# Turning two more attention heads through memory, contracting 128 rows for the others, and storing three results from another queue

## The chip, the cores and the metric

The kernel runs on one core of a Trainium2 chip. Its engines are PE (matmuls; PEld is its weight load), DVE (vector), ACT (scalar), POOL, and SP, which here only issues DMAs. The metric is the device time of one execution in microseconds. Before the change the median of three runs is 1002.09 us (1002.01 to 1003.88).

## The reference

Three layers follow each other, all in float32:

```python
# q, k, v: (4, 8, 576, 64); f: (4, 8, 576)
scores = scale * q @ k.T + (cum[:, None] - cum[None, :])      # cum = cumsum(log f), causal
attn = softmax(scores); o = attn @ v                          # 32 heads
x = o as (2304 tokens, 512)
h = maximum(x @ w_in, 0);  x = (h * h) @ w_out                # 512 -> 2048 -> 512
h = x @ w2_in;  out = (h - tanh(h)) @ w2_out                  # 512 -> 2048 -> 512
```

## The kernel before

**Precision.** Each float32 operand of a matmul is split into a rounded high part and a low rest, and a product is made of three matmuls: high by high, low by high, high by low. So PE runs 7144 matmuls, most of them 128 rows by 128 columns with 288 or 256 columns moving.

**Blocks.** The first MLP works on 8 blocks `j` of 288 tokens, each in 16 steps `i` over the hidden units. A step has 12 matmuls `hp` (line 168), the square of the ReLU on ACT with its rest on POOL or DVE, and, two steps later, 12 matmuls `yp` (line 197). The second MLP (the last stage, lines 1194 to 1480) multiplies by Strassen's scheme: 7 products for 8, with sums before and after. Attention is woven into blocks 0 to 5 so that PE has other matmuls to run.

**Attention in four forms.** Batch 0 (heads 0 to 7) comes in two parts: `first_a` before block 0 and `first_b` inside it. Heads 8 to `UT`-1 = 15 run in `attention()`: a generator that gives *pieces*, nine a head, each a few instructions. A head's scores `s_ps` (lines 538, 539) go to DVE (row minimum), ACT (exponential), POOL (normalising). The tile `P` is then transposed on PE (`trans`, lines 549 to 552: thirteen full transposes and two small ones), split into `PTh` and `PTl` by ACT and DVE, and multiplied with V (lines 609 and 614). 576 keys are 4 chunks of 128 and one of 64; the matmuls of the last chunk and the corner of the first 64 queries contract 64 rows. `advance` hands out pieces by half-steps: `cuts` and `ENDS` say how many by when (58 of the 116 by half-step 28 of block 0, the rest by half-step 26 of block 1).

**Turned heads.** From head `UT` on, DVE transposes blocks of 32 by 32 (`turn`) into `T`, `put` writes `T` to `p_d` in DRAM with four DMAs, and `get` reads it back, rearranged, into `PTl` with four more. ACT then rounds `PTl` to `PTh` (`p_high`), DVE takes the rest in place (`p_low`), and the same products follow (`pv_begin`, `pv_end`); here the rows beyond 64 are zeros and all matmuls contract 128. `plan_head` puts each of these into a *slot*, two to a step. Slot 0 is step 0 of block 2. A head has 7.75 slots (`PERIOD`), the first turned head starts at `START` = -4. At its slot a function runs either before the step's matmuls or, with `behind=True`, after them. The tile `PTl` has one buffer: `get` waits until the head before has been multiplied. Every second head is followed by `store_x` (lines 497, 498), two DMAs of the pair's outputs to `x_d`, from which `load_x` later fetches the tokens of a block.

**Order.** All DMAs but four small ones are issued by SP, in its program order, so one that waits holds up those behind it. For instructions emitted before step `MARK` (step 0 of block 2) the order on each engine is that of a scheduler's first pass; later ones stand as written.

**Before block 0** weights `w1` are widened and split for the first four hidden tiles (`split_a`, `split_b`, at the heads that `SPLIT_A` and `SPLIT_B` name) between the heads of `first_a`. The last pair of heads ends with the rounding of `xhl` (ACT) and its rest (POOL, line 433), which block 0's first step needs.

**The last stage** makes `gq` (DVE, POOL) in two buffers and stores each with one DMA `g_d<-gq` (`h_store`, line 1215). Step n+2 can write only when the store of step n has landed.

Of the kernel before, what the change touches and what calls it, by code (L numbers as in the profile page):

```python
# [16 lines left out]
B, H, S, D = 4, 8, 576, 64  # L17
# [8 lines left out]
LAG = 2  # L26
RING = 3
XLOADS = (((8, 0, 4),), ((11, 0, 3), (13, 3, 4)), ((13, 0, 4),))
F0 = 18
SLK = (None, 8)  # L30
MARK = (2, 0)
BUSY = (34, 2, 4, 6, 4, 0, 0, 0)
UT = 16
ENDS = (28, 26)
PERIOD = 7.75
START = -4
ENG = {
# [7 lines left out]
}  # L45
FETCH = {6: 4, 7: 5, 8: 6}
SPLIT_A = {4: 0, 6: 1, 8: 2, 9: 3}
SPLIT_B = {5: 0, 7: 1, 9: 2, 10: 3}
EARLY_SPLIT = 4
AHEAD_W = 3  # L50
W2EARLY = 6
TB = 288
NG = NF // 2
N2 = 288
# [15 lines left out]
def kernel(  # L70
# [10 lines left out]
    nc = tc.nc  # L81
# [23 lines left out]
    def by(name):  # L105
        return {"A": nc.scalar, "V": nc.vector, "P": nc.gpsimd, "S": nc.sync}[ENG[name]]
# [15 lines left out]
    def rest(eng, out, in_, hi):  # L122
        eng.tensor_tensor(out, in_, hi.bitcast(F32), ALU.subtract)  # L123
# [85 lines left out]
    def latest(engine):  # L209
        return next(x for x in reversed(nc.cur_bb.bb.instructions) if x.engine == engine)  # L210
# [118 lines left out]
    def first(h, part):  # L329
# [76 lines left out]
        def o_step():  # L406
            ps = bank0(part, "o_ps")
            t0 = tiles[0]
            for c in ((0, 2, 3, 4, 1) if part else (0, 2, 1)):
                if c == 4:  # L410
                    nc.tensor.matmul(ps[0:64, 128:256], vr[0:64, 4], ptr[0][:, 0:128], start=False, stop=False)
                    continue
                t = max(t0, c)
                nc.tensor.matmul(ps[0:64, (t - t0) * 128:256], vr[:, c], pt[0][:, c, t - 1:t0 + 1].rearrange("p t j -> p (t j)"),  # L414
                                 start=(c == 0), stop=(c == 1))
            if not part:
                ps0 = bank0(part, "o0_ps")
                nc.tensor.matmul(ps0[0:64, 0:64], vr[0:64, 0], ptr[0][:, 0:64], start=True, stop=True)
            e = h % 2
            if e == 0:  # L420
                XS[0] = two.tile([128, S], F32, tag="xs", name="xs")
            xs = XS[0]
            rr = slice(64 * e, 64 * e + 64)
            c0 = 320 if part else 64
            rounded(by("b_xs" if part else "a_xs"), xs[rr, c0:c0 + 256], ps[0:64, 0:256])
            if not part:
                rounded(by("a_xs0"), xs[rr, 0:64], ps0[0:64, 0:64])
            if e == 1:
                if part:
                    store_x(0, h // 2, xs, 320, S)  # L430
                else:
                    rounded(nc.scalar, X[0][0][:, h // 2], xs[:, :TB])
                    rest(by("a_xl"), X[0][1][:, h // 2], xs[:, :TB], X[0][0][:, h // 2])
                    rounded(nc.scalar, XE[:, 0, h // 2].bitcast(F32R), xs[:, TB:320])
                    rest(nc.gpsimd, XE[:, 1, h // 2], xs[:, TB:320], XE[:, 0, h // 2])
                    if h == H - 1:
                        for a in range(2):
                            nc.sync.dma_start(x_d[0][:, :, a, TB:320].rearrange("k p n -> p k n"), XE[:, a])
# [143 lines left out]
    def pv_parts(u):  # L582
        vh = VH.pop(u)
        b, h = divmod(u, H)
        e = h % 2
        ps = bank(u, "o_ps")
        if u < UT:
            hi, lo = (PT[k].rearrange("p q a s j -> p (q a s j)").rearrange("p (c t j) -> p c t j", c=4, t=4) for k in "hl")
            po = ps.rearrange("p (s j) -> p s j", s=4)
            at = lambda p, c, t: p[0:64, 3, 0] if c == 4 else p[:, c, t:]  # L590
            po_at = lambda t: po[:, t:]
            p0 = lambda p: p[0:64, 3, 1, :64]
            rows = 64
            seq = [(hi, 0), (hi, 1), (lo, 1), (hi, 2), (lo, 2), (hi, 4), (hi, 3), (lo, 3), (lo, 4), (lo, 0)]
        else:
            hi, lo = PT["h"], PT["l"]
            po = ps.rearrange("p (q s j) -> p q s j", q=4, s=4)
            at = lambda p, c, t: p[:, :, 2, 0] if c == 4 else p[:, :, c, t:]
            po_at = lambda t: po[:, :, t:]
            p0 = lambda p: p[:, 0:2, 3, 1]  # L600
            rows = 128
            seq = [(hi, 0), (hi, 1), (hi, 2), (hi, 3), (hi, 4), (lo, 1), (lo, 2), (lo, 3), (lo, 4), (lo, 0)]
        po4 = po[:, 3] if u < UT else po[:, :, 3]

        def products(a, z):
            for n, (pt, c) in list(enumerate(seq))[a:z]:
                t = max(0, c - 1)
                w, o = (vh[0:rows, c], po4) if c == 4 else (vh[:, c], po_at(t))
                nc.tensor.matmul(o, w.rearrange("p a d -> p (a d)"), at(pt, c, t), start=(n == 0), stop=(n == len(seq) - 1))  # L609

        def corner():
            ps0 = PS0[u] = bank(u, "o0_ps")
            for n, (a, p) in enumerate(((0, hi), (1, hi), (0, lo))):
                nc.tensor.matmul(ps0[0:64, 0:64], vh[0:rows, 0, a], p0(p), start=(n == 0), stop=(n == 2))

        xt = one.tile([64, 512], F32, tag="xsh", name="xt")

        def upper():
            rounded(nc.scalar, xt, ps[64:128])

        def out():
            if e == 0:
                XS[0] = two.tile([128, S], F32, tag="xs", name="xs")
            xs = XS[0]
            r = slice(64 * e, 64 * e + 64)
            if u < UT:
                nc.vector.tensor_tensor(xs[r, 64:], ps[0:64], xt, ALU.add)
            else:
                nc.vector.tensor_tensor(
                    xs[r, 64:].rearrange("p (s q j) -> p q s j", s=4, q=4),  # L630
                    ps[0:64].rearrange("p (q s j) -> p q s j", q=4, s=4),
                    xt.rearrange("p (q s j) -> p q s j", q=4, s=4), ALU.add,
                )
            rounded(by(pre(u) + "xs0"), xs[r, 0:64], PS0[u][0:64, 0:64])
            if e == 1:
                store_x(b, h // 2, xs, 0, S)

        return products, corner, upper, out
# [10 lines left out]
    def steady_init():  # L649
        for t in range(5):  # L650
            P[t] = one.tile([128, PT_SZ[t]], F32, tag=f"P{t}", name=f"P{t}")
            if t % 4:
                nc.gpsimd.memset(P[t][:, NKEY[t]:], 0.0)
        PT["h"] = one.tile([128, 4, 4, 4, 32], F32R, tag="PTh", name="PTh")
        PT["l"] = one.tile([128, 4, 4, 4, 32], F32R, tag="PTl", name="PTl")
        PT["t"] = one.tile([128, 4, 4, 4, 32], F32, tag="T", name="T")
        nc.gpsimd.memset(PT["t"], 0.0)

    def attention(u0):
        for p in range(u0 - 2, UT):  # L660
# [94 lines left out]
    def plan(slot, f, *a, behind=False):  # L755
        PLAN.setdefault(slot, ([], []))[behind].append((f, a))

    def plan_head(k):
# [38 lines left out]
        if new:  # L797
            plan(o + 5, turn, 2)
            plan(o + 5, turn, 1)
            plan(o + 5, turn, 0)  # L800
            plan(o + 5, put, k)
            plan(o + 6, get, k, behind=True)
        if k == UT + 1:
            plan(o, prep_v, UT)
        if k + 1 < NU:
# [17 lines left out]
    def weights_early(h):  # L823
        if h in FETCH:
            fetch_w(w1, FETCH[h], FETCH[h])
        if h in SPLIT_B:
            for s in range(2):
                split_b(SPLIT_B[h], s)
        if h in SPLIT_A:
            for s in range(2):  # L830
                split_a(w1, SPLIT_A[h], s, two, "QA", 2)

    TA = one.tile([128, 2048], F32, tag="T", name="TA")
    XE = TA[:, 1024:1280].rearrange("p (a k n) -> p a k n", a=2, k=NK)
    first_a(weights_early)

    def w1_ahead(i):
        if EARLY_SPLIT <= i + AHEAD_W - 1 < NF:
# [258 lines left out]
    later = []  # L1097
    for k in range(UT + 1, NU + 1):
        plan_head(k)
    for g in range(NB * NF + LAG):  # L1100
        j, i = divmod(g, NF)
        if (j, i) == MARK:
# [109 lines left out]
    def h_store(n):  # L1212
        b, g = n // NG, HSEQ[n % NG]
        t = 2 * N2 * b
        nc.sync.dma_start(g_d[g][:, :, t:t + 2 * N2].rearrange("p f (a n) -> p f a n", a=2),
                          GQ.pop(n).rearrange("p (f a) n -> p f a n", f=2))

    YO, GT = {}, {}
# [319 lines left out]
```

## Time and profile before

| | |
|---|---|
| median of three runs | 1002.09 us |
| the profiled execution | 1002.52 us |
| its span on the core | 1000.7 us |
| PE busy | 978.0 us (98%), 7144 matmuls |
| DVE, ACT, POOL busy | 722.6, 615.8, 393.7 us |
| DMA | 211.56 MB, mean 211 GB/s |
| granted PE clock | 0.994 of 2.4 GHz |

The span is the time between the first and the last recorded instruction; 1.8 us of the execution lie around it. PE is shown busy nearly throughout, but matmuls overlap in the records: a matmul's length is longer than the distance to the next one. What a piece of PE's work costs is therefore read here as the distance between starts in a timeline. Block 0 begins at 49 us, block 1 at 165, block 2 at 263; the last stage runs from 629 us to the end.

### The profile page before, as it was taken

How to read it: one execution, taken by the hardware profiler on the slowest of the kernel's cores; microseconds unless marked ns; L12 is line 12 of the kernel's file. 1: busy time of each engine (PE TensorE's matmuls, PEld its weight loads, DVE VectorE, ACT ScalarE, POOL GpSimd, SP SyncE). 2: the span in 40 equal slices, each digit the busy share in tenths (PEclk: the TensorE clock that was granted, in tenths of full speed). 3: DMA queues.
4: the chain of work that ended last, by engine and by line, in shares of the span. 5: the costliest groups of instructions: out<-in, count | busy, mean ns of one | idle time of the engine just before them, and what ended most of it. 6: DMA issues, size and time to landing. Idle time of an engine off the chain costs nothing.

```text
span 1000.7 us, 19994 instructions
## 1 busy us (share of the span) xinstructions
PE 978.0 (98%) x7144; PEld 930.1 (93%) x7144; DVE 722.6 (72%) x1715; ACT 615.8 (62%) x1387; POOL 393.7 (39%) x452
## 2 busy tenths in 40 slices
PE   7989999999999999999999999999999999999998
PEld 6767778888999999999999999999999999999998
DVE  5998774777676878778626577567878787887851
ACT  5988786766686777777657777455566553333330
POOL 4343565455454435454304547146657520000000
PEclk8999999999999999999999999999999999999999
DMA  8646551223657576766547984987776798434351
GB/s 259 256 129 207 174 164 65 92 83 122 202 204 251 205 235 221 248 217 225 195 161 265 348 284 175 396 335 265 273 269 240 252 349 330 148 117 137 127 169 64
DMA packets 91443, 211.56 MB, mean 211 GB/s; under 512 B 9208, under 2 KB 33840, under 8 KB 89040
## 3 DMA queue, kind: packets, MB, share of 16 engines
q1 hardware_dynamic: 91216, 210.29, 60.7%
q8 instruction: 56, 0.92, 0.4%
q14 instruction: 43, 0.35, 0.1%
q10 hardware_dynamic: 128, 0.01, 0.0%
HBM read 132.20 MB, written 78.05 MB: 210 GB/s over the span
## 4 chain that ended last, share of the span: by engine, by line
PE 82%; DVE 6%; DMA 5%; ACT 3%; issue 1%; POOL 1%; SPq 1%; DVEq 0%; POOLq 0%; ACTq 0%
PE yp L197 19%; PE hp L168 19%; PE wp L1279 16%; PE wp L1203 12%; PE o_ps L609 4%; PE wp L1291 2%; DMA g_d<-gq 2%; PE o_ps L414 2%; PE s_ps L373 1%; PE s_ps L702 1%; DVE wt L973 1%; PE s_ps L701 1%; PE t_ps L549 1%; DMA R<-in_qk_dram 1%; PE t_ps L395 1%
## 5 line engine op out<-in xcount | busy, mean ns | idle before, releaser
L168 PE MATMUL hp<-xhl,w 128*128 128x288 f32 x1536 | 234.6, 298 | 3.5 <-ACT xhl L110 1.6
L168 PEld LDWEIGHTS hp<-xhl,w 128*128 128x128 f32 x1536 | 212.6, 189 | 6.8 <-ACT xhl L110 1.8
L197 PE MATMUL yp<-gh,w 128*128 128x288 f32 x1024 | 213.1, 299 | 0.0
L197 PEld LDWEIGHTS yp<-gh,w 128*128 128x128 f32 x1024 | 165.1, 189 | 1.9 <-issue 1.3
L1203 PE MATMUL wp<-xo,wg 128*128 128x288 f32 x1152 | 160.2, 296 | 2.9 <-DVE gq L1210 2.7
L1279 PE MATMUL wp<-go,wg 128*128 128x256 f32 x1344 | 161.4, 283 | 0.0
L1279 PEld LDWEIGHTS wp<-go,wg 128*128 128x128 f32 x1344 | 161.4, 192 | 0.0
L1203 PEld LDWEIGHTS wp<-xo,wg 128*128 128x128 f32 x1152 | 155.5, 189 | 4.2 <-DVE gq L1210 4.1
L197 PE MATMUL yp<-gl,w 128*128 128x288 f32 x512 | 152.2, 297 | 0.6 <-POOL gl L123 0.6
L525 POOL TENSOR_SCALAR P<-P,ST 128x192 f32<-128x192 f32 (+4 forms) x120 | 96.6, 812 | 134.7 <-DVE ST L717 79.3
L110 ACT ACTIVATE go<-gt 128x1792 fp32r<-128x1792 f32 (+1 forms) x34 | 58.3, 1717 | 101.4 <-PE wp L1279 73.3
L514 ACT ACTIVATE P<-P,ST 128x320 f32<-128x320 f32 (+4 forms) x151 | 84.8, 562 | 38.2 <-DVE ST L505 37.8
L505 DVE CUSTOM_DVE_ANT_0 P<-s_ps,mk 128x320 f32<-128x320 f32 (+3 forms) x151 | 63.3, 436 | 61.2 <-PE s_ps L702 33.3
L123 DVE TENSOR_TENSOR gl<-tmp,gh 128x288 fp32r<-128x288 f32 x96 | 60.1, 627 | 53.2 <-ACT tmp L178 52.7
L197 PEld LDWEIGHTS yp<-gl,w 128*128 128x128 f32 x512 | 96.7, 189 | 1.2 <-POOL gl L123 0.8
L123 DVE TENSOR_TENSOR go<-gt,go 128x1792 fp32r<-128x1792 f32 (+1 forms) x34 | 69.6, 2047 | 35.4 <-ACT go L110 32.3
L174 ACT ACTIVATE tmp<-hp 128x288 f32<-128x288 f32 x128 | 51.7, 404 | 58.6 <-PE hp L168 56.5
L123 POOL TENSOR_TENSOR wt<-wt,whi 128x512 f32<-128x512 f32 (+1 forms) x48 | 60.6, 1283 | 59.2 <-ACT whi L110 27.6
L178 ACT ACTIVATE tmp<-tmp 128x288 f32<-128x288 f32 x128 | 56.7, 443 | 3.3
L177 ACT ACTIVATE gh<-tmp 128x288 fp32r<-128x288 f32 x128 | 56.1, 438 | 2.0
L1210 DVE TENSOR_TENSOR gq<-wp,sm 128x288 f32<-128x288 f32 x96 | 40.7, 452 | 17.6 <-ACT sm L1209 10.7
L1341 POOL TENSOR_TENSOR gq<-sm,sm 128x288 f32<-128x288 f32 x32 | 28.6, 893 | 56.0 <-ACT sm L1340 34.8
(167 smaller groups left out, 1720.3 us busy)
## 6 DMA issues: line engine op xcount, KB each, us to landing
wg<-wg_d SPq DMA_DIRECT2D x24, 896.0 KB
g_d<-gq SPq DMA_DIRECT2D x32, 576.0 KB
raw<-in_w_dram SPq DMA_DIRECT2D x16, 1024.0 KB
p_d<-T SPq DMA_DIRECT2D x64, 256.0 KB
PTl<-p_d SPq DMA_DIRECT2D x64, 256.0 KB
raw<-in_w_dram SPq DMA_DIRECT2D x32, 512.0 KB
gt<-g_d SPq DMA_DIRECT2D x32, 512.0 KB
R<-in_qk_dram SPq DMA_DIRECT2D x24, 576.0 KB
```

Of the source, the lines that this page charges most:

```text
L110: eng.activation(out, in_, AF.Copy)
L123: eng.tensor_tensor(out, in_, hi.bitcast(F32), ALU.subtract)
L168: nc.tensor.matmul(ps, w[:, k * 128:(k + 1) * 128], x[:, k], start=(jj == 0), stop=(jj == 11))
L174: nc.scalar.activation(tmp, ps, AF.Relu)
L177: nc.scalar.activation(gh, tmp, AF.Square)
L178: nc.scalar.activation(tmp, tmp, AF.Square)
L197: nc.tensor.matmul(yp[m][:, :n], w[:, c], x, start=(at == 0 and j == 0), stop=(at == NF - 1 and j == 2))
L505: nc.vector.tensor_tensor_reduce(p[:rows, a:b], ps[:rows, :b - a], mk[:rows, o:o + b - a], -0.125, 3.0e38 if mn is None else mn, ALU.add, ...
L514: nc.scalar.activation(p[:rows, :n], p[:rows, :n], AF.Exp, bias=mn, scale=-1.0, accum_out=st[:rows, 1, t:t + 1])
L525: by(n_by).tensor_scalar(p[:rows, :n], p[:rows, :n], st[:rows, 3, t:t + 1], 1.0, ALU.mult, ALU.mult)
L1203: nc.tensor.matmul(ps, wg[:, ws, k * 128:(k + 1) * 128], xo[:, xs, k], start=(i == 0 and first_), stop=(i == 5), skip_group_check=True)
L1279: nc.tensor.matmul(ps, wg[:, ws, m * 128:(m + 1) * 128], YO[n][xs][:, YX[xn]], start=(j == 0 and m == 0 and i == 0), stop=(j == 2 and i == ...
```

## The change

`UT` falls from 16 to 14, so heads 14 and 15 are turned through DRAM, and the plan starts 16 slots earlier, at step 6 of block 1. The pieces of `attention()` fall from 116 to 98: 66 of them in block 0, two handed out before it, the rest by half-step 13 of block 1. The products of heads 8 to 13 contract 128 rows in every matmul; the rows 64 to 127 of that part of `PTh` and `PTl` are set to zero once. `get` moves from behind slot 6 to the front of slot 7, after the outputs of the head before. The weights of the fourth hidden tile are split one head later, and the rest of the last `xhl` goes to DVE (`a_xe`). In the last stage the stores of steps 1 to 3 are issued by ACT. `MARK` moves to step 10 of block 1.

```diff
-F0 = 18
+F0 = 26
-MARK = (2, 0)
+MARK = (1, 10)
-UT = 16
-ENDS = (28, 26)
+UT = 14
+ENDS = (28, 13)
-START = -4
+START = -20
-SPLIT_A = {4: 0, 6: 1, 8: 2, 9: 3}
-SPLIT_B = {5: 0, 7: 1, 9: 2, 10: 3}
+SPLIT_A = {4: 0, 6: 1, 8: 2, 10: 3}
+SPLIT_B = {5: 0, 7: 1, 9: 2, 11: 3}
...
-                    rest(by("a_xl"), X[0][1][:, h // 2], xs[:, :TB], X[0][0][:, h // 2])
+                    rest(by("a_xl" if h < H - 1 else "a_xe"), X[0][1][:, h // 2], xs[:, :TB], X[0][0][:, h // 2])
...
-            at = lambda p, c, t: p[0:64, 3, 0] if c == 4 else p[:, c, t:]
+            at = lambda p, c, t: p[:, 3, 0] if c == 4 else p[:, c, t:]
-            p0 = lambda p: p[0:64, 3, 1, :64]
-            rows = 64
+            p0 = lambda p: p[:, 3, 1, :64]
...
-                w, o = (vh[0:rows, c], po4) if c == 4 else (vh[:, c], po_at(t))
+                w, o = (vh[:, c], po4) if c == 4 else (vh[:, c], po_at(t))
...
+        for k in "hl":
+            x = PT[k].rearrange("p q a s j -> p (q a s j)")[64:128, 1536:1728]
+            rounded(nc.scalar, x, PT["t"][64:128, 0, 0].rearrange("p s j -> p (s j)")[:, :1].to_broadcast([64, 192]))
...
-            plan(o + 6, get, k, behind=True)
+            plan(o + 7, get, k)
...
+        with tc.issue_after(latest(EngineType.Activation)) if h == H + 2 else ExitStack():
...
+    with tc.issue_after(latest(EngineType.Activation)):
+        weights_early(H + 3)
...
+    advance(2)
...
-        nc.sync.dma_start(g_d[g][:, :, t:t + 2 * N2].rearrange("p f (a n) -> p f a n", a=2),
+        (nc.scalar if n in (1, 2, 3) else nc.sync).dma_start(g_d[g][:, :, t:t + 2 * N2].rearrange("p f (a n) -> p f a n", a=2),
```

On PE, at step 10 of block 1, the kernel before runs a head of `attention()`: matmuls `hp` of that step, transposes `t_ps` of P, scores of the next head.

```order
L168 MATMUL hp<-xhl,w_1456 128x288 x12
L549 MATMUL t_ps<-ident,P_1583 128x128 x4
L538 MATMUL s_ps<-QA 128x448
L539 MATMUL s_ps<-QB 128x448
L197 MATMUL yp<-gh,w_1267 128x288 x2
L197 MATMUL yp<-gl,w_1267 128x288
```

In the changed kernel the same step (its weights are `w_1488` there) is followed by the products of head 14, the first turned one.

```order
L168 MATMUL hp<-xhl,w_1488 128x288 x12
L607 MATMUL o_ps<-PTh,VH 128x512 x2
L607 MATMUL o_ps<-PTh,VH 128x4x96
L607 MATMUL o_ps<-PTh,VH 128x4x64
L607 MATMUL o_ps<-PTh,VH 128x4x32
L607 MATMUL o_ps<-PTl,VH 128x512
L607 MATMUL o_ps<-PTl,VH 128x4x96
L607 MATMUL o_ps<-PTl,VH 128x4x64
L607 MATMUL o_ps<-PTl,VH 128x4x32
L607 MATMUL o_ps<-PTl,VH 128x512
L612 MATMUL o_ps<-PTh,VH 64x64 x2
L612 MATMUL o_ps<-PTl,VH 64x64
```

No transpose stands on PE from there on.

On SP, in blocks 2 to 5, at a head that ends a pair: `put` (line 574), `get` (580), the pair's stores (497, 498) and the next head's load (273), before,

```order
L574 DMA p_d_83<-T 128x512 x4
L580 DMA PTl<-p_d_83 32x4x512 x4
L497 DMA x_d_81<-xsh 128x576
L498 DMA x_d_81<-xs 128x576
L273 DMA R<-in_qk_dram 128x1152
```

and now:

```order
L574 DMA p_d_83<-T 128x512 x4
L497 DMA x_d_81<-xsh 128x576
L498 DMA x_d_81<-xs 128x576
L580 DMA PTl<-p_d_83 32x4x512 x4
L273 DMA R<-in_qk_dram 128x1152
```

The four loads of `PTl` have moved behind the two stores; at the other heads, which store nothing, their place is the same.

On ACT at the start of block 0, before: outputs `xs` of the last head of `first_a`, widening of weights (line 146), rounding of `xhl`, and the first ReLU (174).

```order
L110 ACTIVATE xs<-o_ps 64x256
L110 ACTIVATE xs<-o_ps 64x64
L146 ACTIVATE wst<-raw 128x512 x2
L110 ACTIVATE xhl<-xs 128x288
L110 ACTIVATE TA<-xs 128x32
L146 ACTIVATE wst<-raw 128x512
L110 ACTIVATE w_731<-wst 128x512 x2
L174 ACTIVATE tmp<-hp 128x288
```

Now:

```order
L110 ACTIVATE xs<-o_ps 64x256
L110 ACTIVATE xs<-o_ps 64x64
L110 ACTIVATE TA<-xs 128x32
L110 ACTIVATE xhl<-xs 128x288
L146 ACTIVATE wst<-raw 128x512 x2
L174 ACTIVATE tmp<-hp 128x288
```

The rounding of `xhl` has moved ahead of two widenings, and the first ReLU ahead of the splits of `w_731`.

## Rows read from the trace of the kernel before

**Rows 1.** The page, part 4: the chain that ended last, by engine.

```profile
PE 82%; DVE 6%; DMA 5%; ACT 3%; issue 1%; POOL 1%; SPq 1%; DVEq 0%; POOLq 0%; ACTq 0%
```

**Rows 2.** Busy time of engines (instructions), clock, DMA, by stretch.

```profile
49.00:97.00 48.00, 41.84 (x237) 32.39 (x237) 44.20 (x99) 40.24 (x92) 21.97 (x28) 0.96 0.53 162
97.00:165.00 68.00, 66.99 (x407) 52.55 (x406) 46.02 (x148) 49.45 (x119) 34.99 (x49) 1.00 0.46 149
165.00:253.00 88.00, 87.53 (x585) 77.16 (x584) 62.93 (x211) 58.44 (x154) 46.40 (x66) 1.00 0.28 91
300.00:500.00 200.00, 200.00 (x1475) 196.59 (x1474) 155.51 (x420) 146.17 (x363) 93.72 (x103) 1.00 0.66 224
```

**Rows 3.** PE, head in block 1: start, length, line, operation, tiles.

```profile
222.24 0.73 PE L609 MATMUL o_ps<-PTh,VH 128*128 128x512 f32 x2
...
225.25 1.35 PE L168 MATMUL hp<-xhl,w 128*128 128x288 f32 x9
226.44 0.38 PE L549 MATMUL t_ps<-ident,P 128*128 128x128 f32 x2
...
227.03 0.36 PE L538 MATMUL s_ps<-QA 128*128 128x192 f32 x1
...
229.17 0.60 PE L549 MATMUL t_ps<-ident,P 128*128 128x128 f32 x4
229.53 0.39 PE L538 MATMUL s_ps<-QA 128*128 128x320 f32 x1
```

**Rows 4.** Timeline of PE, turned head in block 2.

```profile
281.75 0.97 PE L609 MATMUL o_ps<-PTh,VH 128*128 128x512 f32 x5
282.57 0.48 PE L197 MATMUL yp<-gh,w 128*128 128x288 f32 x2
...
284.21 1.03 PE L609 MATMUL o_ps<-PTl,VH 128*128 128x512 f32 x5
...
285.22 1.82 PE L168 MATMUL hp<-xhl,w 128*128 128x288 f32 x12
```

**Rows 5.** Groups by shape: rows*columns, count | busy, mean ns | idle.

```profile
L538 PE MATMUL s_ps<-QA 128*128 128x320 f32 x18 | 6.6, 367 | 0.0
...
L701 PE MATMUL s_ps<-QA 128*128 128x320 f32 x30 | 9.3, 308 | 0.0
...
L609 PE MATMUL o_ps<-PTh,VH 128*128 128x128 f32 x16 | 3.6, 222 | 0.0
...
L609 PE MATMUL o_ps<-PTh,VH 64*128 64x128 f32 x8 | 2.6, 324 | 0.0
...
L609 PEld LDWEIGHTS o_ps<-PTh,VH 128*128 128x128 f32 x112 | 19.4, 188 | 3.4 <-ACT PTh L110 1.0
...
L609 PEld LDWEIGHTS o_ps<-PTh,VH 64*128 64x128 f32 x8 | 1.5, 183 | 2.0 <-issue 2.0
```

**Rows 6.** Last stage: the chain, then timelines of DVE, PE.

```profile
647.13 10.79 DMA g_d<-gq
...
658.01 1.19 DVE L1210 TENSOR_TENSOR gq<-wp,sm 128x288 f32<-128x288 f32 x3 [3.43 <-DMA g_d<-gq]
...
658.52 3.47 PE L1203 MATMUL wp<-xo,wg 128*128 128x288 f32 x24 [2.13 <-DVE gq L1210]
```

**Rows 7.** Loads of PTl: timelines of SP, POOL, ACT; a wait of ACT.

```profile
286.06 2.99 SPq L580 DMA_DIRECT2D PTl<-p_d  x4
...
287.79 1.45 POOL L123 TENSOR_TENSOR xs<-xs,xsh 128x576 f32<-128x576 f32 x1 [2.27 <-ACT xsh L110]
...
295.42 2.08 ACT L110 ACTIVATE PTh<-PTl 128x512 fp32r<-128x512 f32 x4
...
ACT PTh L110 <- DMA PTl<-p_d: 1.3, 2, 0.9
```

**Rows 8.** Timeline of PE at the first step of block 0.

```profile
53.38 0.53 PE L168 MATMUL hp<-xhl,w 128*128 128x288 f32 x2 [1.56 <-ACT xhl L110]
54.47 0.40 PE L168 MATMUL hp<-xhl,w 128*128 128x288 f32 x1 [0.56 <-POOL xhl L123]
```

More of the change, by code (lines that the diff above doesn't have):

```diff
@@ L600, in pv_parts @@
             p0 = lambda p: p[:, 0:2, 3, 1]
-            rows = 128
             seq = [(hi, 0), (hi, 1), (hi, 2), (hi, 3), (hi, 4), (lo, 1), (lo, 2), (lo, 3), (lo, 4), (lo, 0)]
@@ L613, in corner @@
             for n, (a, p) in enumerate(((0, hi), (1, hi), (0, lo))):
-                nc.tensor.matmul(ps0[0:64, 0:64], vh[0:rows, 0, a], p0(p), start=(n == 0), stop=(n == 2))
+                nc.tensor.matmul(ps0[0:64, 0:64], vh[:, 0, a], p0(p), start=(n == 0), stop=(n == 2))
         xt = one.tile([64, 512], F32, tag="xsh", name="xt")
@@ L825, in weights_early @@
             fetch_w(w1, FETCH[h], FETCH[h])
[L826 to L831, printed above, removed]
+        with tc.issue_after(latest(EngineType.Activation)) if h == H + 2 else ExitStack():
+            if h in SPLIT_B:
+                for s in range(2):
+                    split_b(SPLIT_B[h], s)
+            if h in SPLIT_A:
+                for s in range(2):
+                    split_a(w1, SPLIT_A[h], s, two, "QA", 2)
     TA = one.tile([128, 2048], F32, tag="T", name="TA")
```

2 rows, old and new, of the table ENG are left out of this document.

## Prediction

> **What bounds the kernel now.** I read the chain that ended last first, then the stretches, and only then timelines of the places that the change touches. The chain's shares say that 82% of the span hangs on PE and no other engine holds more than 6% [rows 1]. The stretches say where that is not so [rows 2]. From 300 to 500 us PE has no idle time at all (200.00 of 200.00) while DVE is at 155.51. In the last 68 us of block 0 and the last 88 of block 1 PE is at 66.99 of 68 and 87.53 of 88. Only the first 48 us of block 0 are different: PE is at 41.84, DVE at 44.20, which is 92%. The granted clock is 1.00 of the upper level, 2.4 GHz, in the last three stretches and 0.96 in the first. So nearly everywhere a matmul taken off PE shortens the run by the distance that it put between its neighbours, and work given to DVE, ACT, POOL or the DMA queues costs nothing unless it makes PE wait. The exception is the beginning of block 0, where DVE sets the pace, and there the change puts more work.
>
> The sum is made against the profiled execution: 1002.5 us, a span of 1000.7 and 1.8 around it. The median of the runs is 1002.1, so 0.4 comes off at the end. About 0.2%, 2 us, is what a measurement of this kernel can tell from no change.
>
> **What comes off PE.** *128 rows in the products of heads 8 to 13.* In the trace a head of `attention()` starts its products at 222.24 and the next matmul of the block starts at 225.25: 3.01 us [rows 3]. A turned head in block 2, which multiplies the same tiles but contracts 128 rows everywhere, needs 282.57 − 281.75 and 285.22 − 284.21, together 1.83 us [rows 4]. The changed heads get the same shapes, so I take the whole difference, 1.18, for each of six heads: 7.1 us. The groups by shape show what lies behind it [rows 5]: the matmul of 64 rows has a mean of 324 ns against 222 for the same 128 columns on 128 rows, and PE's loads for it waited 2.0 us in eight of them for nothing that the trace shows, a quarter of a microsecond each. Lower bound: that quarter and the tenth by which the matmul is longer, at the two `o_ps` matmuls of 64 rows in a head (one of `PTh`, one of `PTl`), 0.70, 4.2 in all; upper bound 7.1, which I take, since the three corner matmuls of 64 rows are not in the lower one.
>
> The Trainium skill, "TensorE: Matmul & The Clock Gate", section "LDWEIGHTS (loading the stationary operand)", says that the time of a load is set by its columns and not by the rows contracted, so that 32 rows load as slowly as 128. For the loads the trace agrees: 183 ns with 64 rows, 188 with 128 [rows 5]. By that rule alone 64 and 128 rows cost the same, and of the savings worked out here only 6.4 in 15.9 would come; against it stand the idle time before just these loads and the longer matmuls.
>
> *Heads 14 and 15 are turned.* Their products gain the same 1.18 each, 2.4. Their transposes on PE go: the four of t = 1 are 0.59 us (226.44 to 227.03), four others 0.36 (229.17 to 229.53), so a head has 0.59 + 2 × 0.36 + 3 × 0.09 = 1.58 [rows 3], 3.2 for two. Their scores are issued in the planned form, whose 320-column matmul has a mean of 308 ns against 367 in the other [rows 5]; two heads' worth of scores changes form, and with a few matmuls of such a difference in each I take 0.3 a head, 0.6 (0 to 0.8). Together 6.2.
>
> *Last stage.* The store of step 1 takes 10.79 us to land, DVE's `gq` of step 3 waits 3.43 for it, and PE waits 2.13 for `gq` [rows 6]. It sits on SP's queue behind large loads of `wg`; on ACT's own queue it starts at once. The 16 transfer engines are shared, so it may still be slow: gain 0 to 2.1. What it displaces are weight loads, later by at most one store. I take 2.1, since it needs only two of the 10.8 us.
>
> *Start of block 0.* PE waits 1.56 for ACT's `xhl` and 0.56 for POOL's rest of it [rows 8]. ACT now rounds `xhl` ahead of two widenings and DVE takes the rest. So up to 2.1 goes; but what comes next is the stretch that DVE bounds [rows 2], and most of what PE wins there it will spend waiting for DVE. I take 0.5 (0 to 2.1).
>
> Savings: 7.1 + 6.2 + 2.1 + 0.5 = 15.9.
>
> **What it costs.** *DVE in block 0.* It gets 66 pieces where it had 58: eight more, 0.9 of a head. In the last 88 us of block 1, where some 6.5 heads run, DVE is busy for 62.93 us [rows 2], so a head takes 9.7 of DVE at most (the MLP's part is in it), 8.7 for the 0.9. PE's part of the changed head is 1.83 + 1.58 + about 2 of scores, 5.4, or 4.9 for the 0.9; that is only moved and comes back in block 1. Where DVE is full, the extra pieces thus cost 8.7 − 4.9 = 3.8, and there the 1.18 of the products buy nothing either: 48 of block 0's 116 us hold about 2.4 heads with products, 2.8. Upper end 6.6. Lower end 0: from 97 to 165 us DVE has 22 us idle of 68 [rows 2], and the pieces are spread over the whole block. I take 2, nearer to the lower end because more than half of the block has room; the work that hides the rest is that stretch's PE, at 66.99 of 68.
>
> *`get` behind the stores.* From block 2 on, at every second head the loads of `PTl` are issued after the pair's two stores, whose source `xs` POOL finishes at 287.79 + 1.45 = 289.24, where the loads were issued from 286.06 [rows 7]: 3.2 us later, plus 0.5 for issuing the stores, 3.7. There the loads were all issued by 286.06 + 2.99 = 289.05 and ACT's `p_high` began at 295.42 [rows 7]; between them lie 6.4 us, part of it flight and part slack. In the whole run ACT waited for these loads only twice, 1.3 us together [rows 7], so slack is left at nearly every head; with the middle of 0 and 6.4, 3.2, ACT starts half a microsecond late. The products come in the slots after `p_high`, and a slot is about 3.1 us of PE (98 us of block 1 over 32), which covers it. Behind SP's waiting store stand the next loads of `R` and of weights; they are for later slots. I take 1 us for all eight such heads (0 to 30, without slack and cover), near the lower end because two layers of cover are larger than what is left over.
>
> *The join.* The first turned head now runs inside block 1, and the scheduler's order ends at its step 10. I take the 0.5 of idle that PE has in the 88 us there now [rows 2] once more (0 to 2). The zeroing of rows 64 to 127 is two small ACT instructions long before the first product: nothing.
>
> Costs: 2 + 1 + 0.5 = 3.5. Net −12.4: 1002.5 − 12.4 = 990.1 on the profile's basis, 989.7 on that of the median; I say 989.5.
>
> **Rivals.**
> 1. *DVE becomes the bound of all of block 0.* For it: 92% busy in its first 48 us. Against: 46.02 of 68 in the rest. It costs 6.6 in place of 2: 989.7 + 4.6 = 994.3.
> 2. *The loads behind the stores make PE wait.* The place is the products of the eight heads that end a pair: the stores wait for POOL's `xs`, the loads wait behind them, `p_high` is late, and PE, which runs in order, stands at `o_ps` with the block's matmuls behind it. Without slack and cover that is 3.7 a head, 30 in all: 15.9 − 2 − 0.5 − 30 gives 1019, slower than before. It decides from (15.9 − 2.5) / 8 = 1.7 us a head on. For it: the slack that I took is an estimate from a range of 0 to 6.4. Against: only two short waits of ACT for these loads in 16 heads.
> 3. *Contracted rows cost nothing* The idle before 64-row loads then has another cause, such as the turn from one operand to the next, and stays. For it: the loads themselves are equally long, 183 and 188 ns. Against: the matmuls are not, 324 and 222 ns [rows 5]. The 7.1 + 2.4 don't come: 989.7 + 9.5, 999. The rule of the Trainium skill cited above leads here.
> 4. *All costs are hidden.* For it: DVE's 22 idle us late in block 0 and ACT's slack. Against: the first 48 us. The savings come whole and the start gives 0.5 to 1 more: 1002.1 − 16.6 = 985.5.
>
> **How the numbers follow.** Chances: the forecast with its own range 987 to 992.5, 0.73; rival 1, 0.13; rival 2, 0.05; rival 3, 0.04; rival 4, 0.05. Faster by over 0.2% (below 1000.1) are the forecast, rivals 1 and 4, most of rival 3 and a fraction of rival 2's middle: 0.94. Within 0.2%: 0.02. Slower: 0.04. The range of 8 in 10 or more reaches from 984 (rival 4, with the start's full gain) to 997 (rival 1 with one or two more of the join and of PE's waits at pairs).
>
> **What would show it.** Right if a head's products in block 0 and 1 take 1.8 us from start to start; if no transposes on PE follow after step 6 of block 1 and block 2 starts some 12 us earlier on the span's clock; if PE's wait for `gq` near 650 us is gone; if blocks 2 to 5 keep 100% of PE. The cost on DVE shows as PE idle in the first 50 us of block 0, that of `get` as ACT's waits for `PTl` and PE's for `PTh` at every second head. The forecast is wrong if those waits exceed one microsecond a head, if the 64-row matmuls were not what made the products long, or if block 0 grows by more than the eight pieces' PE work, 5 us, and these 2.

## The result and the profile after

The changed kernel is slower: 1010.45 us median of 9 runs (1006.43 to 1013.31) against 1003.39 us before (1000.91 to 1006.54, 9 runs); ratio 1.0071, 95% interval 1.0055 to 1.0087. The profiled execution of it took 1007.16 us, 1005.4 in its span; it is the second fastest of the nine, so the two profiles show 4.6 of the 7.1 us that lie between the medians.

The chain that ended last, by engine (part 4 of the page of the changed kernel; before in [rows 1]):

```profile
PE 73%; DVE 8%; DMA 8%; ACT 5%; issue 3%; POOL 2%; SPq 1%; DVEq 0%; ACTq 0%; POOLq 0%
```

PE's share is 9 points lower, and DMA, ACT and issue have taken most of them: PE now waits in places. Where, the stretches show (the columns of [rows 2]; the same four stretches of the changed kernel):

```profile
49.00:97.00 48.00, 44.59 (x258) 33.83 (x257) 43.70 (x106) 41.55 (x97) 21.56 (x29) 1.00 0.62 188
97.00:165.00 68.00, 63.85 (x388) 49.78 (x387) 53.02 (x169) 53.30 (x126) 37.23 (x53) 1.00 0.48 158
165.00:253.00 88.00, 84.55 (x573) 78.00 (x572) 56.94 (x183) 58.34 (x146) 47.58 (x65) 0.96 0.39 134
300.00:500.00 200.00, 198.34 (x1423) 190.18 (x1422) 152.75 (x416) 144.02 (x358) 82.31 (x102) 1.00 0.63 215
```

The first 48 us of block 0, where I had put the risk, got better (PE 44.59 for 41.84). The end of block 0 got worse, block 1 has a granted clock of 0.96, and from 300 to 500 us PE issues 1423 matmuls where it issued 1475. Busy time hardly tells of this (198.34 of 200), since the lengths in the records overlap and cover short waits. The count does.

From the starts of the first `hp` of each block (before in the same way) come the lengths below. The last stage is from its first matmul to PE's last.

| kernel | before block 0 | block 0 | block 1 | blocks 2 to 5 | last stage |
|---|---|---|---|---|---|
| before | 48.9 | 115.8 | 97.8 | 260.6 | 367.7 |
| changed | 49.6 | 120.2 | 90.6 | 269.4 | 365.7 |

Block 1 and the last stage gain 9.2, block 0 and blocks 2 to 5 lose 13.2.

What the change was to take off PE, it took off in the main. The products of one head with 128 rows, in block 1 (start, length, line, operation, tiles; the changed lines 607 and 612 are 609 and 614 of before; compare [rows 3]):

```profile
176.12 0.63 PE L607 MATMUL o_ps<-PTh,VH 128*128 128x512 f32 x2
...
178.00 0.44 PE L549 MATMUL t_ps<-ident,P 128*128 128x128 f32 x2
```

1.88 us from the first product to the next matmul (1.87 to 2.31 for the six heads), 3.01 before (2.81 to 3.11 for its eight). Then, in blocks 2 to 5, SP's timeline and a part of ACT's at a head that ends a pair (compare [rows 7]):

```profile
282.91 1.80 SPq L574 DMA_DIRECT2D p_d<-T  x4
286.39 0.32 SPq L497 DMA_DIRECT2D x_d<-xsh  x1
287.91 0.32 SPq L498 DMA_DIRECT2D x_d<-xs  x1
288.33 2.55 SPq L580 DMA_DIRECT2D PTl<-p_d  x4
```

```profile
296.41 2.09 ACT L110 ACTIVATE PTh<-PTl 128x512 fp32r<-128x512 f32 x4 [2.06 <-DMA PTl<-p_d]
```

SP stands at the first store until 286.39 and at the second until 287.91, and only then come the loads. ACT waits 2.06 us for them. PE meets the roundings at that pace (compare [rows 4]):

```profile
297.14 1.85 PE L607 MATMUL o_ps<-PTh,VH 128*128 128x512 f32 x5
298.83 0.48 PE L197 MATMUL yp<-gh,w 128*128 128x288 f32 x2
```

Five matmuls that took 0.82 us from the first to the next `yp` take 1.69, because the four roundings of `PTh` take 2.09 and PE has begun 0.73 after their start (in the kernel before 2.7 after). ACT's waits for these loads, in the whole run (us in all, times, longest):

```profile
ACT PTh L110 <- DMA PTl<-p_d: 16.9, 12, 2.3
```

They were 1.3 in two times [rows 7]. Not every head is hit: the five products, always 0.81 or 0.82 us in blocks 2 to 5 of the kernel before, take 1.05 to 1.69 in ten of the sixteen heads there and are unchanged in the other six.

### The profile page after: what moved, and what is told of

It is laid out like the page before. It is cut to its first block, busy times and chain, and to the rows that moved or that the text cites. A ratio compares the mean times of both kernels' runs of the same rounds, so it can differ in the third digit from the quotient of the medians.

```text
span 1005.4 us, 19949 instructions
## 1 busy us (share of the span) xinstructions
PE 978.7 (97%) x7114; PEld 927.4 (92%) x7114; DVE 718.5 (71%) x1712; ACT 620.9 (62%) x1387; POOL 381.5 (38%) x453
## 4 chain that ended last, share of the span: by engine, by line
PE 73%; DVE 8%; DMA 8%; ACT 5%; issue 3%; POOL 2%; SPq 1%; DVEq 0%; ACTq 0%; POOLq 0%
PE wp L1284 16%; PE hp L168 16%; PE yp L197 15%; PE wp L1208 13%; PE o_ps L607 4%; DMA R<-in_qk_dram 3%; PE wp L1296 2%; DMA PTl<-p_d 2%; PE o_ps L414 1%; PE s_ps L373 1%; DVE wt L977 1%; PE s_ps L703 1%; PE s_ps L702 1%; DMA g_d<-gq 1%; SPq L580 1%
## 5 line engine op out<-in xcount | busy, mean ns | idle before, releaser
L525 POOL TENSOR_SCALAR P<-P,ST 128x192 f32<-128x192 f32 (+4 forms) x118 | 84.0, 722 | 116.8 <-DVE ST L718 79.1
L123 DVE TENSOR_TENSOR gl<-tmp,gh 128x288 fp32r<-128x288 f32 x96 | 58.0, 605 | 57.0 <-ACT tmp L178 56.5
L123 DVE TENSOR_TENSOR PTl<-PTl,PTh 128x512 fp32r<-128x512 f32 x72 | 44.6, 671 | 17.5 <-ACT PTh L110 17.5
L1215 DVE TENSOR_TENSOR gq<-wp,sm 128x288 f32<-128x288 f32 x96 | 41.2, 453 | 16.9 <-ACT sm L1214 11.3
```

The costliest lines, as they stand in the source:

```text
L525: by(n_by).tensor_scalar(p[:rows, :n], p[:rows, :n], st[:rows, 3, t:t + 1], 1.0, ALU.mult, ALU.mult)
```

## Experiments

The theories. A: the loads of `PTl` behind the stores cost what blocks 2 to 5 lost. B: it is the plan's phase, by which half of the turned heads lie a slot earlier. C: where PE waits, the granted clock falls, and the wait costs more than its length. D: the saving of the 128 rows reaches the end; E: DVE takes it back. F: block 0 grows by the work moved into it and by waits for DVE. G: at the join, where the last head of `attention()` hands over to the plan and the first head is turned, the stores hold up that head too. Times are medians; the lengths of blocks and of the last stage come from one profiled run each, which need not lie at the median (`fill_join` and `back_64` were profiled in their slowest run). The first four kernels, the next four and the last four ran on three different chips, where the kernel before stood at 1003.2, 1002.6 and 1002.1. The times of single runs spread over 5 to 11 us in most kernels; differences under 2 us are not read. Between groups, differences of medians and of the ratios differ by up to 1.4 us.

| run | time | ratio to before, 95% | block 0 | block 1 | blocks 2 to 5 | last stage |
|---|---|---|---|---|---|---|
| get_back | 1002.19 | 0.9990 (0.9969–1.0012) | 122.0 | 88.1 | 264.4 | 365.1 |
| get_only | 1010.69 | 1.0067 (1.0041–1.0092) | 114.8 | 98.2 | 268.0 | 367.4 |
| rows_stores | 1003.29 | 0.9991 (0.9970–1.0011) | 119.1 | 94.2 | 261.4 | 369.1 |
| fill_join | 1015.30 | 1.0114 (1.0083–1.0146) | 122.4 | 91.5 | 269.9 | 372.6 |
| back_64 | 1005.51 | 1.0030 (1.0007–1.0052) | 124.8 | 95.5 | 263.0 | 365.9 |
| back_sp | 1004.78 | 1.0023 (1.0006–1.0040) | 123.9 | 91.2 | 262.9 | 368.4 |
| back_f18 | 1005.00 | 1.0030 (1.0012–1.0047) | 114.9 | 100.7 | 262.3 | 365.1 |
| join_early | 998.42 | 0.9958 (0.9942–0.9974) | 121.5 | 86.2 | 263.8 | 365.3 |
| phase | 996.15 | 0.9921 (0.9897–0.9945) | 120.8 | 85.0 | 260.8 | 365.8 |
| phase_f22 | 1000.67 | 0.9982 (0.9963–1.0001) | 117.7 | 93.7 | 260.9 | 367.9 |
| phase_64 | 1000.78 | 0.9978 (0.9958–0.9997) | 125.5 | 87.3 | 262.1 | 365.1 |
| phase_act | 993.93 | 0.9905 (0.9881–0.9929) | 121.2 | 85.1 | 262.1 | 364.8 |

**get_back**, on the changed kernel:

```diff
-            plan(o + 7, get, k)
+            plan(o + 6, get, k, behind=True)
```

> The changed kernel with one line undone: the loads of PTl are issued behind slot 6 again, ahead of the pair's stores; two more heads turned, 128 rows, stores on ACT's queue all stay. Theory A (the loads behind the stores land too late, and PE waits at the products): blocks 2 to 5, 269.4 us in the changed kernel and 260.6 before, fall to 260 to 262; the products of a head at the end of a pair start at least 2 us after the first rounding of PTh; time about 1000 to 1001. Rival B (it is the plan's phase, START = -20 in place of -4, by which half of the heads lie a slot earlier): blocks 2 to 5 stay at 268 to 270, time 1009 to 1011.

8.3 us faster than the changed kernel; its profile has blocks 2 to 5 shorter by 5.0 (264.4; 262.3 to 263.8 in the next kernels with the same plan) and block 1 by 2.5. The latter is hardly the loads' doing: the join is as in the changed kernel, but in this profile the granted clock does not fall there (rows under join_early). SP at a like head:

```profile
281.83 1.80 SPq L574 DMA_DIRECT2D p_d<-T  x4
284.02 3.20 SPq L580 DMA_DIRECT2D PTl<-p_d  x4
287.27 0.58 SPq L497 DMA_DIRECT2D x_d<-xsh  x1
```

The loads go 2.2 us after the writes, not 5.4; ACT rounds at 293.13 and PE's product, at 295.83, needs 0.98 us for its five. Theory A, with something left over in blocks 2 to 5: 2 to 4 us above before.

**get_only**, the opposite of that line on the kernel before.

> The kernel before with the one line changed: the loads of PTl go to the front of slot 7, behind the pair's stores; all else as before. Theory A: blocks 2 to 5 grow by 6 to 9 us from 260.6, PE shows waits for PTh at every second head, time 1010 to 1012. Rival B (phase): under 2 us of growth, time 1003 to 1005.

7.5 us slower, all of it in blocks 2 to 5 (268.0 for 260.6), with the old phase. Theory A is shown from both sides: the one line, moved in either kernel, is worth 7.5 to 8.3 us. B can only be the rest.

```profile
300.74 1.86 PE L609 MATMUL o_ps<-PTh,VH 128*128 128x512 f32 x5 [0.26 <-issue]
302.43 0.48 PE L197 MATMUL yp<-gh,w 128*128 128x288 f32 x2
```

This is PE in that kernel: the same 1.69 us for five matmuls as in the changed one.

**rows_stores**, on the kernel before, 128 rows as in the diff and ACT's queue for the stores of g 1 to 3.

> The kernel before with 128 rows contracted in the products of heads 8 to 15 and the stores of g 1 to 3 on ACT's queue; the plan, the pieces and the loads of PTl as before. If the matmuls of 64 rows are what made these products long, each falls from 2.97 us to 1.85 to 2.1, blocks 0 and 1 together from 213.7 to 205 to 207, the last stage shortens by 2, and the time is 993 to 995. Rival (in blocks 0 and 1 other engines take back what PE wins): the products shorten but blocks 0 and 1 lose 4 us at most; 998 to 1000.

Both theories missed: no gain that can be measured, although all products together fell from 53.0 to 46.1 us. In blocks 0 and 1, where a scheduler orders the instructions, shorter products changed the order, and PE came to wait for the sums that free a bank of PSUM (`s_ps<-QA` for DVE's `xs`: 3.5 us in five waits, none in the kernel before):

```profile
157.57 0.30 PE L538 MATMUL s_ps<-QA 128*128 128x64 f32 x1 [1.44 <-DVE xs L627]
```

Around it the granted clock is below its upper level (the columns of [rows 2]; the first two rows are of this kernel):

```profile
142.00:146.00 4.00, 4.00 (x21) 4.00 (x20) 2.33 (x15) 2.50 (x9) 2.49 (x5) 0.57 0.53 196
...
158.00:162.00 4.00, 3.98 (x22) 3.70 (x22) 2.66 (x14) 2.36 (x9) 1.58 (x4) 0.68 0.44 152
```

```profile
142.00:146.00 4.00, 4.00 (x31) 3.79 (x31) 3.04 (x15) 3.88 (x12) 2.82 (x6) 1.00 0.99 340
...
158.00:162.00 4.00, 3.98 (x31) 3.78 (x30) 2.31 (x8) 2.54 (x6) 0.94 (x2) 1.00 0.05 19
```

The second two are of the kernel before: 31 matmuls where 21 are now. The four microseconds up to 142 us show PE at 2.69 of 4 and those up to 158 at 2.56. The last stage, too, was 1.4 longer in this profile: the one wait of 2.13 at 658 us is gone, and five of 0.25 to 0.79 for `gq` have come. So the run does not tell D from E; a kernel with fewer waits is needed.

**fill_join**, on the changed kernel, before the products of the first turned head:

```diff
+            if a == 0 and u == UT:
+                for _ in range(24):
+                    nc.tensor.matmul(ps[:, :128], ident, ident, start=True, stop=True)
```

> The changed kernel with 24 matmuls of 128 columns more, whose results are overwritten, ahead of the products of the first turned head in block 1, where PE waited 0.95 us for PTh and the granted clock was 0.50 from 230.6 to 237.5 us. Theory C (PE's idle time there made the clock fall): no stretch under 1.00 between 225 and 245 us, block 1 shorter by 2.5 to 3.5 us, time 1007 to 1008. Rival (the clock falls for another reason): block 1 longer by 0.3 to 1.4 us, the lower clock stays, 1010 to 1012.

In the changed kernel, block 1 around the join:

```profile
226.00:230.00 4.00, 3.00 (x18) 2.13 (x16) 1.20 (x2) 2.00 (x5) 0.81 (x1) 1.00 0.87 262
230.00:234.00 4.00, 3.84 (x16) 2.87 (x16) 1.94 (x7) 2.37 (x6) 1.28 (x2) 0.58 1.04 401
234.00:238.00 4.00, 4.00 (x17) 3.91 (x18) 1.57 (x5) 1.61 (x4) 0.38 (x1) 0.57 0.75 267
```

and with the fill:

```profile
228.00:232.00 4.00, 4.00 (x37) 4.00 (x36) 0.61 (x2) 0.00 (x0) 0.00 (x0) 1.00 0.81 250
232.00:236.00 4.00, 4.00 (x33) 4.00 (x31) 0.88 (x2) 2.73 (x6) 0.80 (x1) 1.00 1.01 365
236.00:240.00 4.00, 3.84 (x23) 2.95 (x22) 2.99 (x8) 2.69 (x7) 1.28 (x2) 1.00 0.48 192
```

The clock does what theory C says: almost no idle time on PE, 1.00 throughout. The time does not: 1015.30, 4.9 slower than the changed kernel. The fill itself is 5.3 us of matmuls (the trace has 48 of 0.11), and it stands 10 us ahead of the products (226.01 to 231.28; the products start at 236.13), so it delays PE until the loads have landed more than it fills a gap. Block 1 is 0.9 longer and the last stage 6.9, with waits of PE for `gq` of up to 2.05; why these grew is not shown. The remedy was dearer than the ill, and one profile does not show that the idle time caused the fall: `get_back` has the same idle time at the join and stays at the upper level (its rows stand under join_early).

**back_64**, on get_back, `rows = 64` for heads 8 to 13 as before the change.

> The version with the loads of PTl ahead of the stores (median 1002.2, against 1003.2 before), with the products of heads 8 to 13 back on 64 rows for the last chunk and the corner. In the trace 128 rows took 0.9 us off a head's products. Theory D (that time reaches the end): blocks 0 and 1 longer by 4 to 6 us, time 1006 to 1008. Rival E (in blocks 0 and 1 DVE, which frees the banks of PSUM, takes it back): blocks 0 and 1 within 2 us, time 1001 to 1004.

3.3 us slower, between the theories; the intervals of this kernel and of `get_back` overlap.

**back_sp**, on get_back, all stores `nc.sync`.

> The version with the loads of PTl ahead of the stores, and all stores of the last stage on SP's queue again. If ACT's queue is what took away PE's wait of 2.1 us for gq: a wait near 657 us is back, the last stage 2 us longer, time 1004. Rival (the last stage's waits move from run to run with the DMA traffic: 1.4 us more in one profile with ACT's queue, 2.0 less in others): within 1 us of 1002.

2.6 us slower, with intervals that just overlap. The wait is back, PE for DVE, and its releaser on DVE's timeline:

```profile
660.85 3.46 PE L1208 MATMUL wp<-xo,wg 128*128 128x288 f32 x24 [1.47 <-DVE gq L1215]
```

```profile
660.34 1.19 DVE L1215 TENSOR_TENSOR gq<-wp,sm 128x288 f32<-128x288 f32 x3 [3.52 <-DMA g_d<-gq]
```

**back_f18**, on get_back, `F0 = 18`.

> The version with the loads of PTl ahead of the stores, with 58 pieces of attention() in block 0, as before the change, and 40 in block 1. Theory F (block 0's 6.2 us more are 3.9 of moved matmuls and 2.2 of waits for DVE, and block 1's waits come from the turned heads): block 0 falls to 115 to 117, block 1 grows from 88.1 by 4 to 5, time 1000 to 1003. Rival (40 pieces in half of block 1 are too many for DVE and the first turned head is late): block 1 over 96, time 1005 to 1010.

The rival, at the lower edge of its range: block 0 is back at 114.9, block 1 at 100.7, of which the join has its part (from 230 to 234 us PE is busy for 0.29 of 4). Moving pieces out of block 0 does not pay.

**join_early**, on get_back, in `attention()` at the last head:

```diff
-                pv(p)
+                products, corner, upper, out = pv_parts(p)
+                products(0, 10)
+                corner()
+                upper()
+                if p + 1 < UT:
+                    out()
             if p + 1 == UT:
                 turn(1)
                 turn(0)
                 put(UT)
                 get(UT)
+                out()
```

> The version with the loads of PTl ahead of the stores, and the same done for the first turned head in block 1: the sums of head 13's outputs and its stores come after the writes and loads of head 14 on DVE's and SP's queues. Theory G (at the join the stores hold up p_d and PTl in the same way; PE waited 1.16 us and then at the pace of ACT's roundings): the loads are issued 3 us earlier, the first product waits for nothing, block 1 shorter by 1.5 to 2.5 us, time 999 to 1001. Rival (the loads are early but ACT or DVE is late, since the sums free a bank of PSUM later): block 1 within 1 us or longer, 1002 to 1004.

Theory G: 3.8 us faster than get_back by the medians, 3.2 by the ratios; 1.9 of it is block 1 of the two profiles. SP and PE at the join:

```profile
216.80 1.79 SPq L574 DMA_DIRECT2D p_d<-T  x4
219.01 2.90 SPq L580 DMA_DIRECT2D PTl<-p_d  x4
221.96 0.58 SPq L497 DMA_DIRECT2D x_d<-xsh  x1
```

```profile
229.60 0.99 PE L607 MATMUL o_ps<-PTh,VH 128*128 128x512 f32 x5
230.42 1.51 PE L607 MATMUL o_ps<-PTl,VH 128*128 128x512 f32 x5
```

The changed kernel has there, with the loads issued from 220.94 after one of the writes had stood behind the stores:

```profile
228.82 1.90 PE L607 MATMUL o_ps<-PTh,VH 128*128 128x512 f32 x5 [0.95 <-ACT PTh L110]
230.56 1.88 PE L607 MATMUL o_ps<-PTl,VH 128*128 128x512 f32 x5
```

The clock is up, this time without a fill:

```profile
230.00:234.00 4.00, 3.82 (x22) 2.80 (x22) 2.88 (x10) 2.16 (x6) 1.67 (x2) 1.00 0.98 302
234.00:238.00 4.00, 4.00 (x33) 4.00 (x33) 2.78 (x12) 1.81 (x5) 0.00 (x0) 1.00 1.03 378
```

33 matmuls in the second stretch where the changed kernel issued 17. But this kernel was made from `get_back`, whose profile has the changed kernel's wait at the join (0.99 us for `PTh`) and no fall of the clock behind it:

```profile
226.00:230.00 4.00, 2.99 (x20) 2.44 (x18) 0.63 (x2) 1.94 (x5) 0.80 (x1) 1.00 0.90 237
230.00:234.00 4.00, 3.80 (x17) 2.45 (x18) 2.88 (x8) 3.02 (x7) 1.13 (x2) 1.00 1.05 389
234.00:238.00 4.00, 4.00 (x32) 3.96 (x31) 2.81 (x14) 1.52 (x4) 0.54 (x1) 1.00 0.88 321
```

So the earlier loads take the wait away; that they also keep the clock up is not shown. The runs lie closer together, too: 996.9 to 999.0 in six, against 998.2 to 1005.7 in twelve for get_back.

The order at the join was not made by the change. The kernel before has it at its own join, at the end of block 1:

```profile
254.37 0.55 SPq L497 DMA_DIRECT2D x_d<-xsh  x1
255.85 0.32 SPq L498 DMA_DIRECT2D x_d<-xs  x1
256.22 0.90 SPq L574 DMA_DIRECT2D p_d<-T  x2
257.23 3.22 SPq L580 DMA_DIRECT2D PTl<-p_d  x4
```

There PE's products start at 266.91, 12.5 us after the first store, and wait for nothing; in the changed kernel they start 10.3 us after it (218.52 to 228.82), 0.95 of which is their wait.

**phase**, on join_early, the plan from head 17 on (the products of head 16 are in it) at the slots of before:

```diff
-        o = START + int(PERIOD * (k - UT - 1))
+        o = START + int(PERIOD * (k - UT - 1)) if k < UT + 3 else START + 16 + int(PERIOD * (k - UT - 3))
```

> The version with the join mended (median 998.4), with the slots of heads 16 to 31 as in the kernel before (most of them one slot, 3 us, later than in the changed kernel). In blocks 2 to 5 that version still has 263.8 us against 260.6 before, with four heads in and near block 2 whose products go at the pace of ACT's roundings (2.7 for 1.83 us). Theory H (a slot less between the loads and the products is why): blocks 2 to 5 at 260 to 261.5, three of the four products back at 1.83, time 995 to 996.5. Rival (it is the DMA traffic of block 2, which came with the earlier heads): blocks 2 to 5 within 1 us of 263.8, time 998 to 999.

Theory H, which is B's share: blocks 2 to 5 at 260.8, the time 2.3 less by the medians, 3.7 by the ratios. Of the four paced products, 2.67 to 2.71 us in join_early, three are now at 1.83, 2.08 and 2.51; the fourth, head 15's, whose slot is the same, is still at 2.71.

**phase_f22**, on phase, `F0 = 22`.

> The same with 62 in place of 66 pieces of attention() in block 0 and 36 in place of 32 in block 1. Theory (block 0's waits for DVE grow with the pieces, 2 us for eight): blocks 0 and 1 together shorter by 0 to 1.5 us than in the version with 66 pieces; time 0 to 1.5 less. Rival (DVE in block 1 is the tighter place, as with 40 pieces, where block 1 grew by 12.6): longer by 2 to 6.

4.5 us slower: the rival. In the profiles block 1 is 8.7 longer (93.7 for 85.0) and the last stage 2.1, and block 0 is 3.1 shorter.

**phase_64**, on phase, 64 rows for heads 8 to 13.

> The first kernel of this group with the products of heads 8 to 13 on 64 rows again, the worth of the 128 rows by itself where nothing else waits. On the other version it measured 3.3 us in the time, 6.0 in the distances on PE. Theory D: 4 to 6 us longer than with 128 rows, 1000 to 1002. Rival E (DVE takes half back): 2 to 3.5 us longer, 998 to 999.5.

4.6 us slower, as theory D had it. With fewer waits about, most of what the rows save is seen in the time; the runs of the two kernels spread over 5 and 9 us, so a smaller share, E's, is not excluded.

**phase_act**, on phase:

```diff
-        (nc.scalar if n in (1, 2, 3) else nc.sync).dma_start(g_d
+        (nc.scalar if n else nc.sync).dma_start(g_d
```

> The first kernel of this group with the stores of all steps of the last stage but the first on ACT's queue. PE still waits for gq at 678, 701, 724, 747, 770 us, 0.28 to 0.95 each, 2.3 in all, behind stores that are on SP's queue. If SP's queue is the cause there too: the last stage shorter by 1 to 2 us. Rival (the transfers themselves take 9 us on busy engines whatever the queue): within 0.7 us.

The waits for `gq` are gone; what is left of PE's waits in that stage is

```profile
PE wp L1214 <- POOL xs L123: 0.6, 3, 0.2
```

The last stage is 1.0 shorter and the time 2.2 less, at the edge of what can be told. At 993.93 us, 0.9905 of before, this is the best version.

## Why the prediction was wrong, step by step

*`get` behind the stores* is the step that failed by the most: I took 1 us, it costs 7.5 (get_only) to 8.3 (get_back). The mechanism stood in the prediction as rival 2, with a chance of 0.05, and its sign came, ACT waiting for these loads for 16.9 us in twelve waits. By itself it would not have turned the sum: with 8.3 in place of 1 the forecast would be 997, still faster than before. The rest are the terms below.

The delay was right: the loads go 5.42 us after the first write where they went 2.20 after it, 3.2 later. My two layers of cover were too thin. Of the 3.2 us of slack I had taken the middle of an interval; ACT's rounding came 13.5 us after the first write instead of 11.6, so 1.9 of the delay went through and the slack was about 1.3. The other layer, a slot of PE's matmuls behind the rounding, was in the old trace 2.7 us long (295.42 to 298.1) and not 3.1, and little of it was cover: PE needs the last of four roundings, which take 2.09. With 0.73 of lead left, PE stood three more times within the head shown, and its five products took 0.87 us longer. I had asked when the first quarter is ready, and not when the last is. ACT's own two waits said little about slack: in the old trace ACT was busy right up to the rounding (with `tmp<-hp`, 0.41 us from 295.11), so how long the loads had lain ready does not show there.

*The join* was taken at 0.5 and cost 3.2 to 3.8. The trace of the changed kernel has it: the stores of the pair that head 13 ends stand in front of the last write of head 14 and its loads on SP. The kernel before has the same order at its join, where it made no product wait; I looked at neither. In the changed kernel's profile the lower clock behind the wait comes on top; what makes it fall is open.

*A step that was missing*: START falls by 16 slots where two heads take 15.5, so seven of the fifteen heads from 17 on come a slot earlier than before, and the others where they were. 2.3 us in the time, 3.0 in blocks 2 to 5. I had no term for it.

*128 rows*: 7.1 for six heads; in the changed kernel the six have a mean of 2.07 us, against 2.97 for the eight of before, 5.4 for six, and 4.6 of these reach the end (phase_64). In rows_stores, with heads and plan as before, 128 rows shortened the products as well. Rival 3 is refuted. The Trainium skill, "TensorE: Matmul & The Clock Gate", section "LDWEIGHTS (loading the stationary operand)", speaks of the load's own time, and there the old trace agrees, 183 and 188 ns [rows 5]; it is the wait before these loads and the longer matmuls that went.

*Heads 14 and 15*: the transposes' 3.2 came (30 matmuls fewer, 2.9 us of distances on PE, 12.5 to 9.6). The 2.4 of the products did not: they took 3.70 and 2.71 us at the join. The 0.6 of the scores did not come: the distances behind the score matmuls of heads 8 to 31, waits included, sum to 43.3 us before and to 45.2 in `phase`.

*Last stage*: 2.1 predicted, 2.0 shorter in the changed kernel, 2.6 in time by back_sp. The size was right, and the wait near 658 us is gone wherever steps 1 to 3 store from ACT (and, with all stores on SP, in get_only's profile too). But a later wait for `gq` came in its place (1.23 in the changed kernel, 0.51 to 2.07 in others), and with the same queues rows_stores, fill_join and phase_f22 have 367.9 to 372.6 in this stage. So part of the agreement is luck; only phase_act, with all later stores on ACT, has no wait for `gq` left.

*Start and DVE in block 0*: the wait of 1.56 for `xhl` fell to 0.57 and POOL's 0.56 is gone. Block 0 grew by 4.4, against the 5 of moved work and 2 of waits that I had allowed. The size was right and the place was not: it is the last third, where from 147 to 164 us DVE is busy for 14.53 of 17 (9.48 before) and PE for 14.90 (16.97 before).

Sum: with the three costs that were too small (8.3, 3.8, 2.3) mended, the kernel is at 996.15, 6 us under before by the medians and 8 by the ratio, where 15.9 less 2 for DVE had been expected. 4.7 to 5.5 of the difference are the products and the scores (7.1 + 2.4 + 0.6 against 4.6 to 5.4). That leaves 0.4 to 3.2 us, hardly more than these measurements can tell; which of the small waits in blocks 0 and 1 it is was not tried.

## What to carry to other kernels

When a transfer is moved on a queue, follow it to the last instruction that needs its last part, and compare the delay with what each step on the way can hide, measured at that last part: here 1.3 us before ACT and about 1 before PE, of 3.2. How seldom an engine waits for the transfer does not give its slack. Put stores, which wait for results, behind loads that the next step needs, at every place where the two meet, the seams of a plan included. Read a saving on a saturated engine as worth its full length only where nothing else is close behind: 6.9 us off the products gave nothing that can be measured in rows_stores, and 5.4 us gave 4.6 between phase_64 and phase.

## What was not expected of the hardware

A wait of PE can cost more than its length. At the join of the changed kernel PE was busy for 3.00 of 4 us, in the next 8 us the granted clock was 0.58 and 0.57 of 2.4 GHz, that is mostly at the lower level of 1.2, and each three matmuls `yp` (`gh`, `gh`, `gl`) started 0.72 us after the three before, where it is 0.40 at the upper level. In rows_stores the falls came behind stretches with PE at 2.69 and 2.56 of 4. But not every such stretch is followed by a fall: in get_back PE was busy for 2.99 of 4 at the same place, and the clock stayed at 1.00. What decides between the two is not shown here, nor is it shown that the fill or the earlier loads kept the clock up. The times go with the clock: the nine runs of the changed kernel have mean clocks of 0.988 to 0.995, and the slowest of them, 1013.31, the lowest.
